# Turned spectra held in two Y tiles and one Z tile, moved within the next batch's first steps, with pd later and one x load behind a store

## The chip, the cores and the metric

The kernel runs on one core of one Trainium2 chip. The metric is the device time of one execution in microseconds (us). Before the change it is 518.89 us, the median of three runs (518.23 to 520.21).

## The reference

For each of B = 8 batches of 2496 tokens x 256 channels: a real FFT along the tokens, a complex linear layer on the spectrum, a soft threshold, and the inverse FFT. All 19,968 tokens then go through a soft mixture of experts with 32 slots.

```python
X = np.fft.rfft(x, axis=1)
Xr, Xi = (X.real.astype(np.float32), X.imag.astype(np.float32))
Yr = Xr @ w_r - Xi @ w_i + b_r
Yi = Xr @ w_i + Xi @ w_r + b_i
lam = 0.01
Yr = np.sign(Yr) * np.maximum(np.abs(Yr) - lam, 0.0)
Yi = np.sign(Yi) * np.maximum(np.abs(Yi) - lam, 0.0)
y = np.fft.irfft(Yr + 1j * Yi, n=2496, axis=1)          # becomes x below
logits = x @ phi                                        # 32 slots
slot_input = softmax(logits, axis=0).T @ x              # over all tokens
h = relu(slot_input[e] @ w1[e]); slot_out[e] = h @ w2[e]  # 8 experts, 4 slots each
out = softmax(logits, axis=1) @ slot_out
```

## The kernel before, in words

The FFT of length 2496 is split as 39 x 64. Each batch passes three stages, and the stages of neighbouring batches are interleaved on all engines.

- **a-units** (`a_unit`, 11 per batch). TensorE (PE) does the transform of length 39 on x. ScalarE (ACT) makes the high part `xh` of x, GpSimd (POOL) the low part `xl`, and three matmuls make `pa`. ACT copies it to `ast`, and four stores per batch bring it to DRAM (`adr`). The units of batch b run while batch b-1 is in its steps. Loads of x (`xr`, four columns each) go ahead of them.
- **steps** (`f2`, `lin_k`, `lin_y`, `tp_p`; five per batch, 40 in all). A step reads one fifth of `adr` back (`ap`), does the transform of length 64 (`px`), splits it (`xsm`, `xsh`, `xsl`, `xth`, `xtl`), does the linear layer (`pk`, `py`) and the threshold. The result `rt` (two per step, four buffers) goes to the logits (`pq`, `p_sb`).
- **chain of a batch** (`c_stages`, in the batch after). Logits back to tokens (`pg`, the round trip `gd`, `gp` through DRAM, `pL`), maxima, exponentials, then the slot weights back to the spectrum (`pe`, round trip `ed`, `eb`), and `pd`, whose halves need the split `chpd` (ACT) and `clpd` (POOL) of `eb`; `dd` is pd scaled. `slots_acc` then multiplies dd by the spectrum (`pr`).

For `pr` the spectrum is needed with frequency on the partitions. In the first three steps of a batch DVE transposes each `rt` in 32 x 32 blocks into `z` (tile Z, two buffers), and `z_move` sends 16 transfers of 96 KB from Z to `y` (tile Y, one buffer), which finish the turn. The two remaining steps are turned by PE (`pt`, `T`).

The order of the work is written by hand. Every piece is a generator that yields a planned time in units (four units are a step, 20 a batch), and a heap runs the pieces in the order of these times; each engine's instructions, and the transfers on SyncE's queue (SP), then stand in that order. The numbers come from the table `PLAN`: `zo` delays the transposes into z, `zd` and `z6` place the moves, `pd` places pd, `T_['wl']` the loads of the expert weights. All loads and stores in question go through the one queue of SP, in order.

After the 40 steps come the last batch's chain, the experts (`hps`, `po`) and the output (`pq` with `ost`, 41 stores).

Of the kernel before, what the change touches and what calls it, by code (L numbers as in the profile page):

```python
# [23 lines left out]
S = 32  # L24
# [40 lines left out]
def _constants():  # L65
# [87 lines left out]
    "pb": 9.8,  # L153
    "pe": [11.35, 12.35],
    "cm": 14.3,
    "pd": [17.12, 17.75],
    "pr": [20.48, 20.49, 24.48, 24.49, 28.49],
    "au": [1.4, 18.85, 19.7],
    "tho": 1.4,
# [72 lines left out]
def fourier_soft_moe_kernel(ctx: ExitStack, tc: tile.TileContext, t: dict, out: bass.AP):  # L232
# [159 lines left out]
    def a_unit(b, g, u):  # L392
# [170 lines left out]
    def lin_y(s, e):  # L563
        b, grp = steps[s]
        end = s == ns - 1
        t0 = 4 * s + 1 + (PLAN["T_"]["ye"] if end else 1.35) * e
        yield t0
        py = psum("pl", f"py{b}_{grp}_{e}")
        lin(py, e, 0, xts[(s, 0)], 4 * 64 if grp else WH)
        if e == 1 and not end:  # L570
            t0 = 4 * s + 3
            yield t0
        lin(py, e, 1, xts[(s, 1)], 4 * 64 if grp else WH)
        t0 += 0.55 if e == 0 else PLAN["T_"]["yt"] if end else 0.3
        yield t0
        ks = kss[s]
        ut = wtile([128, KG, 2, 64], F32, "ut", f"ut{b}_{grp}_{e}")
        for ri in range(2):
            V.scalar_tensor_tensor(
                out=ut[:, :, ri, :],  # L580
                in0=py[:, ri * 256 : ri * 256 + 256].rearrange("p (j q) -> p j q", q=64),
                scalar=bcol[:, ri, e : e + 1],
                in1=ks[:, e, :].rearrange("p (j q) -> p j q", q=64),
                op0=ALU.add, op1=ALU.add,
            )
        if s >= NZ + 2:
            rt = part("Z", 2, f"rt{b}_{grp}_{e}").rearrange("p (j c q) -> p j c q", c=2, q=64)
        else:
            rt = wtile([128, KG, 2, 64], F32, "rt", f"rt{b}_{grp}_{e}")
        yield t0 + (PLAN["T_"]["th"][e] if end else PLAN["tho"])  # L590
        relu = s < PLAN["hA"] or L_("th", s, e) is A
        if relu:
            A.activation(out=rt, in_=ut, func=AF.Relu, bias=nlam)
        else:
            P.tensor_scalar(out=rt, in0=ut, scalar1=LAM, scalar2=-LAM, op0=ALU.min, op1=ALU.max)
        yield t0 + (PLAN["T_"]["tl"][e] if end else PLAN["tlr" if relu else "tlo"])
        if relu:
            V.scalar_tensor_tensor(out=rt, in0=ut, scalar=LAM, in1=rt, op0=ALU.add, op1=ALU.min)
# [49 lines left out]
    def tp_t(s, h):  # L648
# [396 lines left out]
    def load_w(loc, layer):  # L1045
# [6 lines left out]
        if loc in "ZT":  # L1052
# [399 lines left out]
```

## Time and profile before

| | us |
|---|---|
| median of 3 runs | 518.89 (518.23 to 520.21) |
| profiled execution, its own time | 516.14 |
| its span, first to last instruction | 514.3 |
| PE busy | 489.8 (95%) |
| DVE busy | 358.0 (70%) |
| ACT busy | 328.8 (64%) |
| POOL busy | 311.7 (61%) |

Busy time is summed over one execution. A row of the timeline gives start and length of an instruction (or of several alike in a run), engine, line, operation, what it writes and reads, and in brackets the time its engine sat idle before it with what ended that. The line numbers are those of helpers that record most instructions, so the rows are told apart by the tiles' names, printed without batch numbers. A matmul's row is longer than the time to the next one's start, since matmuls are pipelined.

### The profile page before, as it was taken

The page shows a single profiled execution, that of the slowest core. Times are in us where ns is not written, and L with a number is a line of the kernel's source. Part 1 is how long each engine was busy: PE and PEld are TensorE (multiplying, and loading weights), DVE is VectorE, ACT ScalarE, POOL GpSimd, SP SyncE. Part 2 cuts the span into 40 slices and gives each one's busy share as a digit, 9 for nine tenths or more (in the row PEclk, how much of TensorE's full clock was granted, in tenths as well). Part 3 has the DMA queues.
Part 4 walks back from the last instruction along what each step waited for, and adds up shares of the span by engine and source line. Part 5 has one row for each costly group of instructions (what it writes and reads, how often), then busy time and mean ns, then how long its engine had stood idle before and what let it go on. Part 6 is the DMA issues. An engine that isn't in the chain of part 4 may idle for free. (4 is left out here: it accounts for less than half of the span.)

```text
span 514.3 us, 11973 instructions
## 1 busy us (share of the span) xinstructions
PE 489.8 (95%) x4348; PEld 418.7 (81%) x4348; DVE 358.0 (70%) x706; ACT 328.8 (64%) x718; POOL 311.7 (61%) x361
## 2 busy tenths in 40 slices
PE   8899999999999999999999999999999988999991
PEld 4487999999888978998898998989889866468881
DVE  3257876679667966887689868876896685437671
ACT  4357667768766876687668766775565456147771
POOL 0047587868985788689858985797367423313210
PEclk9899999999999999999999999999999999999997
DMA  8899656489857886888588867965889889939998
GB/s 291 281 322 352 215 185 205 125 260 244 282 127 249 237 273 151 259 237 291 146 258 244 264 169 210 259 233 162 243 203 337 219 244 385 349 121 397 403 406 346
DMA packets 90318, 130.98 MB, mean 255 GB/s; under 512 B 40188, under 2 KB 61692, under 8 KB 90260
## 3 DMA queue, kind: packets, MB, share of 16 engines
q1 hardware_dynamic: 89316, 128.10, 78.3%
q10 hardware_dynamic: 944, 2.13, 1.3%
q8 instruction: 34, 0.56, 0.4%
q14 instruction: 24, 0.20, 0.1%
HBM read 69.19 MB, written 50.00 MB: 232 GB/s over the span
## 5 line engine op out<-in xcount | busy, mean ns | idle before, releaser
L228 POOL TENSOR_TENSOR xl<-xr,xh 117x512 fp32r<-117x512 f32 x73 | 97.2, 1332 | 17.8 <-ACT xh L228 10.2
L304 PEld LDWEIGHTS px<-smov,ap 128*128 128x128 f32 x640 | 80.5, 192 | 6.3 <-issue 1.1
L304 PE MATMUL px<-smov,ap 128*128 128x128 f32 x640 | 84.2, 275 | 1.0 <-DMA ap<-adr 1.0
L228 DVE SCALAR_TENSOR_TENSOR ut<-py,pk,k 128x256 f32<-128x256 f32 x160 | 69.5, 475 | 19.6 <-PE py L304 17.4
L228 POOL TENSOR_TENSOR xsl<-xsm,xsh 128x256 fp32r<-128x256 f32 x77 | 72.1, 937 | 6.3
L228 POOL CAST xsh<-xsm 128x256 fp32r<-128x256 f32 x78 | 35.4, 453 | 66.5 <-DVE xsm L228 53.2
L228 ACT COPY ast<-pa 128x512 f32<-128x512 f32 x82 | 48.3, 591 | 35.4 <-PE pa L304 34.1
L228 DVE TENSOR_TENSOR xsm<-px,xsm 128x256 f32<-128x256 f32 x80 | 33.3, 417 | 40.0 <-ACT xth L228 35.4
L228 DVE TENSOR_TENSOR xtl<-px,xth 128x512 fp32r<-128x512 f32 x80 | 54.3, 679 | 0.1
L304 PE MATMUL py<-xth,nwsh 128*128 128x256 f32 (+1 forms) x160 | 52.9, 331 | 0.4 <-ACT k L228 0.4
L228 ACT CAST xth<-px 128x512 fp32r<-128x512 f32 x80 | 47.3, 592 | 5.4 <-PE py L304 5.3
L228 ACT CAST xh<-xr 117x512 fp32r<-117x512 f32 x72 | 45.3, 631 | 3.8 <-DMA xr<-in_x 3.8
L304 PE MATMUL pk<-xsh,w_rh 128*128 128x256 f32 (+1 forms) x160 | 47.6, 298 | 0.0
L228 POOL TENSOR_TENSOR rt<-ut,rt 128x512 f32<-128x512 f32 x36 | 46.3, 1285 | 0.1
L304 PE MATMUL pk<-xsl,w_rh 128*128 128x256 f32 (+1 forms) x160 | 45.0, 281 | 0.5 <-POOL xsl L228 0.3
L304 PE MATMUL py<-xth,wdh 128*128 128x256 f32 (+1 forms) x160 | 44.9, 281 | 0.0
L304 PE MATMUL py<-xtl,nwsh 128*128 128x256 f32 (+1 forms) x160 | 44.8, 280 | 0.0
L304 PE MATMUL py<-xtl,wdh 128*128 128x256 f32 (+1 forms) x160 | 44.7, 280 | 0.0
L304 PE MATMUL py<-xth,nwsl 128*128 128x256 f32 (+1 forms) x160 | 44.7, 279 | 0.0
L304 PE MATMUL pk<-xsh,w_rl 128*128 128x256 f32 (+1 forms) x160 | 44.7, 279 | 0.0
L304 PE MATMUL py<-xth,wdl 128*128 128x256 f32 (+1 forms) x160 | 44.6, 279 | 0.0
L228 ACT COPY xsm<-px 128x256 f32<-128x256 f32 x80 | 30.0, 375 | 22.6 <-PE px L304 15.2
(223 smaller groups left out, 1298.7 us busy)
## 6 DMA issues: line engine op xcount, KB each, us to landing
ap<-adr SPq DMA_DIRECT2D x76, 256.0 KB
out<-ost SPq DMA_DIRECT2D x37, 512.0 KB
xr<-in_x SPq DMA_DIRECT2D x35, 512.0 KB
adr<-ast SPq DMA_DIRECT2D x20, 768.0 KB
y<-z SPq DMA_DIRECT2D x112, 96.0 KB
w<-in_moe_w SPq DMA_DIRECT2D x21, 512.0 KB
adr<-ast SPq DMA_DIRECT2D x7, 512.0 KB
w<-in_moe_w SPq DMA_DIRECT2D x14, 256.0 KB
```

The source lines that it names most:

```text
L228: return lambda *a, **k: self.tc.keep_in_program_order(f(*a, **k))
L304: tc.keep_in_program_order(nc.tensor.matmul(**kw))
```

## The change

Z gets one buffer and Y two. The moves of a batch no longer wait for the next batch's middle: they stand at 14.9 to 26.6 units after the batch's start (before: 31 to 43.1; in batch 6 at 30.5 to 35). The first step's transposes into z come later (5.25 and 4.0 units instead of 2.2 and 0.7). `pd` moves from 17.12 and 17.75 to 18.9 and 19.2 in batches 0 to 4; batch 5 had these places already. The second load of x of a batch moves from 6 to 4.55 units ahead of its unit. Two weight loads go into Y (14.2 and 13.6 units before the end of the steps) instead of Z (6 and 5.9), the other loads of the table shift by up to 1.8 units, and small tiles at the end are taken from Y instead of Z or the other way round.

```diff
-    "pd": [17.12, 17.75],
+    "pd": [18.9, 19.2],
...
-    "zo": [2.2, 0.7, 1.0],
+    "zo": [5.25, 4.0, 0.7, 1.0],
...
-    "z6": [30.5, 0.3],
...
-    "zd": [31, 31.55, 32.1, 32.65, 33.2, 33.75, 34.3, 34.85, 35.4, 35.95, 36.5, 37.05, 41, 41.7, 42.4, 43.1],
+    "zd": [14.9, 15.4, 15.9, 21.2, 21.65, 22.1, 22.55, 23.0, 23.45, 23.9, 24.35, 24.8, 25.25, 25.7, 26.15, 26.6],
...
-    chain_bufs = {"ap": 3, "xth": 3, "xtl": 3, "xsh": 3, "xsl": 3, "Z": 2, "Y": 1, "T": 8, "p_sb": 2, "g_sb": 1,
+    chain_bufs = {"ap": 3, "xth": 3, "xtl": 3, "xsh": 3, "xsl": 3, "Z": 1, "Y": 2, "T": 8, "p_sb": 2, "g_sb": 1,
...
-            yield PLAN["x1"].get((b, g), tu - 6)
+            yield PLAN["x1"].get((b, g), tu - (4.55 if b > 1 and g == 4 else 6))
...
-            yield 20 * b + (PLAN["zd"][n] if b < B - 2 else PLAN["z6"][0] + PLAN["z6"][1] * n)
+            yield 20 * b + PLAN["zd"][n]
...
-            yield t0 + PLAN["tlo"] + PLAN["zo"][0 if grp == e == 0 else e + 1]
-            if grp == 0 and e == 0:
+            yield t0 + PLAN["tlo"] + PLAN["zo"][2 * (grp > 0) + e]
+            if b not in zts:
...
-            T = part("Z", 2, f"T{b}_{grp}_{h}")
+            T = part("Y", 2, f"T{b}_{grp}_{h}")
...
-            z = part("Z", 4, f"cin{b}")[:, : G * S].rearrange("p (g s) -> p g s", s=S)
+            z = part("Z" if b == 4 else "Y", 4, f"cin{b}")[:, : G * S].rearrange("p (g s) -> p g s", s=S)
```

What this does to the order shows at three places. In the rows below a name is the tile, its batch, and its column or step; the last number only tells buffers apart.

POOL, where pd of batch 4 meets the a-units of batch 7 (`xl7_14` is the low part for unit 14). Before:

```order
L228 TENSOR_TENSOR xl7_12_5074<-xr7_12_4913,xh7_12_5073 117x512
L228 TENSOR_TENSOR clpd4_0_5090<-eb4_4988,chpd4_0_5089 128x320
L228 TENSOR_TENSOR clpd4_1_5127<-eb4_4988,chpd4_1_5126 128x320
L228 TENSOR_SCALAR rt6_0_0_5080<-ut6_0_0_5077 128x512
L228 CAST xsh6_1_1_5119<-xsm6_1_1_5118 128x256
L228 TENSOR_TENSOR xsl6_1_1_5120<-xsm6_1_1_5118,xsh6_1_1_5119 128x256
L228 TENSOR_TENSOR rt6_0_0_5080<-ut6_0_0_5077,rt6_0_0_5080 128x512
L228 TENSOR_TENSOR dd4_4991<-dd4_4991,pk1_111 128x320
L228 TENSOR_TENSOR xl7_14_5164<-xr7_12_4913,xh7_14_5163 117x512
L228 TENSOR_TENSOR dd4_4991<-dd4_4991,pk1_111 128x320
```

Now:

```order
L227 TENSOR_TENSOR xl7_12_5082<-xr7_12_4921,xh7_12_5081 117x512
L227 TENSOR_SCALAR rt6_0_0_5088<-ut6_0_0_5085 128x512
L227 CAST xsh6_1_1_5124<-xsm6_1_1_5123 128x256
L227 TENSOR_TENSOR xsl6_1_1_5125<-xsm6_1_1_5123,xsh6_1_1_5124 128x256
L227 TENSOR_TENSOR rt6_0_0_5088<-ut6_0_0_5085,rt6_0_0_5088 128x512
L227 TENSOR_TENSOR xl7_14_5159<-xr7_12_4921,xh7_14_5158 117x512
L227 TENSOR_TENSOR clpd4_0_5178<-eb4_4996,chpd4_0_5177 128x320
L227 TENSOR_TENSOR clpd4_1_5197<-eb4_4996,chpd4_1_5196 128x320
L227 CAST xsh6_2_0_5207<-xsm6_2_0_5206 128x256
L227 TENSOR_TENSOR xsl6_2_0_5208<-xsm6_2_0_5206,xsh6_2_0_5207 128x256
L227 TENSOR_TENSOR dd4_4999<-dd4_4999,pk1_111 128x320
L227 TENSOR_TENSOR xl7_16_5252<-xr7_16_5075,xh7_16_5251 117x512
```

Both `clpd` and the first `dd` have gone from ahead of `xl7_14` to behind it. On PE the six matmuls of pd go the same way: the first three now stand between `pt` and `py` of the next step, the others behind that `py`, all ahead of the matmuls that read `xl7_14`.

SP, from the last store of batch 6's `adr` to the second fifth read back. Before:

```order
L298 DMA xr7_4_4590<-in_x 128x1024
L298 DMA adr6_3768<-ast6_18_4559 128x1024
L298 DMA y4_4645<-z4_3597 32x768 x4
L298 DMA ap6_0_4735<-adr6_3768 64x4x256 x2
L298 DMA y4_4645<-z4_3597 32x768
L298 DMA xr7_8_4748<-in_x 128x1024
L298 DMA y4_4645<-z4_3597 32x768 x2
L298 DMA ap6_1_4809<-adr6_3768 64x4x256 x2
```

Now:

```order
L297 DMA adr6_3783<-ast6_18_4575 128x1024
L297 DMA xr7_4_4659<-in_x 128x1024
L297 DMA ap6_0_4747<-adr6_3783 64x4x256 x2
L297 DMA xr7_8_4759<-in_x 128x1024
L297 DMA ap6_1_4818<-adr6_3783 64x4x256 x2
L297 DMA y5_4821<-z5_4537 32x768 x3
```

The store stands ahead of the load, and seven moves of batch 4 have left this place.

SP, in the last batch's steps, up to the round trip `gd6`, with loads of expert weights (`w`) between. Before:

```order
L298 DMA ap7_3_5909<-adr7_4592 64x4x256 x2
L298 DMA c_dr5_129<-cb5_5786 128x704
L298 DMA w5_5923<-in_moe_w2 128x1024
L298 DMA w6_5994<-in_moe_w2 128x1024
L298 DMA ap7_4_6034<-adr7_4592 64x4x256 x2
L298 DMA w7_6044<-in_moe_w2 128x1024
L298 DMA w8_6065<-in_moe_w2 128x1024
L298 DMA gd6_6072<-g_sb6_6001 64x20x32 x2
```

Now:

```order
L297 DMA ap7_3_5919<-adr7_4607 64x4x256 x2
L297 DMA y6_5619<-z6_5359 32x768
L297 DMA w5_5930<-in_moe_w2 128x1024
L297 DMA c_dr5_129<-cb5_5794 128x704
L297 DMA y6_5619<-z6_5359 32x768 x2
L297 DMA w6_5990<-in_moe_w2 128x1024
L297 DMA y6_5619<-z6_5359 32x768 x3
L297 DMA ap7_4_6050<-adr7_4607 64x4x256 x2
L297 DMA w7_6053<-in_moe_w2 128x1024
L297 DMA y6_5619<-z6_5359 32x768
L297 DMA w8_6074<-in_moe_w2 128x1024
L297 DMA gd6_6089<-g_sb6_6016 64x20x32 x2
```

Seven moves of batch 6 stand here that stood behind `gp6` before; six more stand between `eb5` and these rows, where four of batch 5 stood. Behind `gp6` all 16 moves are gone.

## Rows read from the trace of the kernel before

**Rows 1.** The page: busy time, share of the span, instructions.

```profile
PE 489.8 (95%) x4348; PEld 418.7 (81%) x4348; DVE 358.0 (70%) x706; ACT 328.8 (64%) x718; POOL 311.7 (61%) x361
```

**Rows 2.** Waits of PE: us in total, times, longest.

```profile
PE pa L304 <- POOL xl L228: 2.8, 4, 0.9
...
PE pr L304 <- DMA y<-z: 1.1, 1, 1.1
PE px L304 <- DMA ap<-adr: 1.0, 1, 1.0
```

**Rows 3.** Timeline of PE: start, length, engine, line, operation, [idle before it].

```profile
34.57 0.50 PE L304 MATMUL pa<-xl,f1h 117*128 117x512 f32 x1 [0.89 <-POOL xl L228]
...
341.24 0.40 PE L304 MATMUL pa<-xh,f1h 117*128 117x512 f32 x1
342.42 0.50 PE L304 MATMUL pa<-xl,f1h 117*128 117x512 f32 x1 [0.78 <-POOL xl L228]
```

**Rows 4.** Timelines of ACT and POOL ahead of that wait.

```profile
333.81 0.46 ACT L228 CAST chpd<-eb 128x320 fp32r<-128x320 f32 x1 [1.00 <-DMA eb<-ed]
...
334.34 0.87 POOL L228 TENSOR_TENSOR clpd<-eb,chpd 128x320 fp32r<-128x320 f32 x1 [1.33 <-ACT chpd L228]
...
340.64 1.73 POOL L228 TENSOR_TENSOR xl<-xr,xh 117x512 fp32r<-117x512 f32 x1
```

**Rows 5.** Timelines of PE and SP around the wait for ap.

```profile
317.37 1.13 PE L304 MATMUL px<-smov,ap 128*128 128x128 f32 x8 [0.98 <-DMA ap<-adr]
...
304.44 0.38 SPq L298 DMA_DIRECT2D adr<-ast  x1
304.91 3.58 SPq L298 DMA_DIRECT2D y<-z  x4
312.68 1.32 SPq L298 DMA_DIRECT2D ap<-adr  x2
```

**Rows 6.** Timelines of PE and DVE where pr of batch 6 begins.

```profile
425.49 1.50 PE L304 MATMUL pr<-y,dd 128*32 128x256 f32 x24 [1.13 <-DMA y<-z]
...
427.79 1.44 PE L304 MATMUL pL<-gp,pk 128*117 128x352 f32 x4
...
424.66 0.97 DVE L228 STREAM_TRANSPOSE gp<-gT 128x352 f32<-128x352 f32 x2
```

**Rows 7.** The chain of waits there: start, us, what.

```profile
420.69 4.57 DMA y<-z
```

**Rows 8.** Timelines of PE and POOL around pd of a batch without waits.

```profile
237.79 0.60 PE L646 MATMUL pt<-pk,rt 128*128 128x128 f32 x4
...
239.65 0.40 PE L304 MATMUL pa<-xh,f1h 117*128 117x512 f32 x1
239.88 0.39 PE L304 MATMUL pa<-xl,f1h 117*128 117x512 f32 x1
...
234.92 1.25 POOL L228 TENSOR_TENSOR xsl<-xsm,xsh 128x256 fp32r<-128x256 f32 x1
...
238.07 1.29 POOL L228 TENSOR_TENSOR xl<-xr,xh 117x512 fp32r<-117x512 f32 x1
```

**Rows 9.** Stretches: busy time of the engines, granted clock, DMA share, GB/s.

```profile
390.00:395.00 5.00, 5.00 (x67) 4.15 (x66) 2.11 (x5) 2.08 (x5) 4.31 (x7) 1.00 1.05 396
...
480.00:490.00 10.00, 10.00 (x55) 8.25 (x55) 7.34 (x12) 7.27 (x17) 2.32 (x3) 1.00 1.02 403
```

**Rows 10.** Timelines of SP and ACT around the round trip gd, gp of batch 6.

```profile
396.11 1.71 SPq L298 DMA_DIRECT2D gd<-g_sb  x2
...
405.43 0.24 ACT L228 COPY gp<-gp 40x64 f32<-40x64 f32 x1 [2.21 <-DMA gp<-gd]
```

**Rows 11.** Timelines of SP, DVE and POOL where z is next written.

```profile
239.39 0.33 SPq L298 DMA_DIRECT2D xr<-in_x  x1
...
248.12 0.71 DVE L228 STREAM_TRANSPOSE z<-rt 128x512 f32<-128x512 f32 x1 [1.94 <-POOL rt L228]
...
250.90 1.28 POOL L228 TENSOR_TENSOR xl<-xr,xh 117x512 fp32r<-117x512 f32 x1
```

More of the change, by code (lines that the diff above doesn't have):

```diff
@@ L168 @@
     "ws": [-29, -28.9, -28.8, 2],
-    "late": {'6': {'cms': [13.1, 13.2, 18, 22.65, 22.66, 22.67], 'pd': [16.681, 16.6], 'pdt': ('pl', 'pl'), 'pr': [17.15, 18.3, 20.179, 19.707, 19.902], 'pL': [6.6, 7.3], 'pm': 8.51, 'pmr': 9.35, 'pb': 10.36, 'pe': [11.747, 11.96, 12.419], 'pg': [0.875, 1.275], 'fr': {'sinv': 0, 'm2': 0, 'f1': 0, 'suni': 0}, 'pbx': 1.2, 'pet': ('pf', 'pf'), 'so': 0.2}, '5': {'pd': [18.9, 19.2], 'so': 1.5}, '4': {}},
-    "T_": {'wl': [[-31, 't', 1], [-29.5, 't', 1], [-27.7, 't', 1], [-25.5, 't', 1], [-23.7, 't', 1], [-21.7, 't', 2], [-20.2, 't', 2], [-19.2, 't', 2], [-18.7, 't', 2], [-18.2, 't', 2], [-15.2, 't', 2], [-14.3, 't', 2], [-13.4, 't', 2], [-12.5, 'c', 2], [-11.8, 's', 1], [-11.2, 'a', 1], [-10.6, 'a', 1], [-10, 'a', 1], [-9.5, 'Ww_r', 1], [-8.7, 'Wnws', 1], [-8.6, 'Wwd', 1], [-6, 'Z', 1], [-5.9, 'Z', 1], [0.01, 'k', 1], [0.01, 'u', 1], [0.02, 'x', 2], [0.02, 'x', 2], [0.02, 'x', 2], [1.4, 'R', 2], [1.4, 'R', 2], [1.73, 'Z', 2], [1.74, 'Z', 2]], 'cl': 2.0, 'cp': 46.5, 'ct': 46.6, 'du': [[2.55, 2]], 'd1': [], 'cm': [19.9, 19.91, 19.92, 25, 25.1, 25.2], 'cm7': [0.71, 1.7, 1.95, 2.7, 2.71, 2.8], 'ye': 0.2, 'te': [[5.6, 0.2], [5.5, 0.4]], 'pg': [-15.49, -11.49, -7.99, -3.934, -2.9], 'yt': 0.578, 'wr': -30.6, 'tp': [0, 0.6, 0.85, 0.5], 'tt': [0.4, 0.55, 0.821, 1.25, 0.994], 'z': 1.686, 'th': [0.1, 0.12], 'tl': [0.24, 0.25], 'pgt': ['ps', 'ps', 'ps', 'pf', 'pf'], 'ch': [0.263, 0.5, 0.7, 1.0, 1.514, 2.0], 'te7': 'AAAAAAAAAA', 'op': 2, 'ot': [3, 5, 7], 'gt': [-14.5, -10.5, -7.0, -3.93, -2.89]},
@@ new lines @@
+    "late": {'6': {'cms': [13.1, 13.2, 18, 22.65, 22.66, 22.67], 'pd': [16.681, 16.6], 'pdt': ('pl', 'pl'), 'pr': [17.15, 18.3, 20.179, 19.707, 19.902], 'pL': [6.6, 7.3], 'pm': 8.51, 'pmr': 9.35, 'pb': 10.36, 'pe': [11.747, 11.96, 12.419], 'pg': [0.875, 1.275], 'fr': {'sinv': 0, 'm2': 0, 'f1': 0, 'suni': 0}, 'pbx': 1.2, 'pet': ('pf', 'pf'), 'so': 0.2}, '5': {'so': 1.5}, '4': {}},
+    "T_": {'wl': [[-31, 't', 1], [-29.5, 't', 1], [-27.7, 't', 1], [-25.5, 't', 1], [-23.7, 't', 1], [-22, 't', 2], [-21, 't', 2], [-19.5, 't', 2], [-18.9, 't', 2], [-18.3, 't', 2], [-16.2, 't', 2], [-15.5, 't', 2], [-14.8, 't', 2], [-14.2, 'Y', 1], [-13.6, 'Y', 1], [-12.5, 'c', 2], [-11.8, 's', 1], [-11.2, 'a', 1], [-10.6, 'a', 1], [-10, 'a', 1], [-9.5, 'Ww_r', 1], [-8.7, 'Wnws', 1], [-8.6, 'Wwd', 1], [0.01, 'k', 1], [0.01, 'u', 1], [0.02, 'x', 2], [0.02, 'x', 2], [0.02, 'x', 2], [1.4, 'R', 2], [1.4, 'R', 2], [1.73, 'Z', 2], [1.74, 'Z', 2]], 'cl': 2.0, 'cp': 46.5, 'ct': 46.6, 'du': [[2.55, 2]], 'd1': [], 'cm': [19.9, 19.91, 19.92, 25, 25.1, 25.2], 'cm7': [0.71, 1.7, 1.95, 2.7, 2.71, 2.8], 'ye': 0.2, 'te': [[5.6, 0.2], [5.5, 0.4]], 'pg': [-15.49, -11.49, -7.99, -3.934, -2.9], 'yt': 0.578, 'wr': -30.6, 'tp': [0, 0.6, 0.85, 0.5], 'tt': [0.4, 0.55, 0.821, 1.25, 0.994], 'z': 1.686, 'th': [0.1, 0.12], 'tl': [0.24, 0.25], 'pgt': ['ps', 'ps', 'ps', 'pf', 'pf'], 'ch': [0.263, 0.5, 0.7, 1.0, 1.514, 2.0], 'te7': 'AAAAAAAAAA', 'op': 2, 'ot': [3, 5, 7], 'gt': [-14.5, -10.5, -7.0, -3.93, -2.89]},
@@ L1051, in load_w @@
             src = t["moe_w2"][e, h * 512 : h * 512 + 512, :].rearrange("(p f) d -> p (f d)", f=4)
-        if loc in "ZT":
+        if loc in "YZT":
             parts = [part(loc, 4, f"w{i}")]
```

## The prediction, on record before the changed kernel was timed

> **What bounds the kernel now.** I read the page's busy times first. PE works 489.8 us [rows 1] of a span of 514.3, so no change of order can be worth more than the 24.5 us in which it stands, and much of that lies in the start and behind the last matmul. None of PE's work changes: the two orders hold the same matmuls. So the question is which of PE's waits the change removes and which it makes. The second view is the table of PE's waits: three of its rows name something that the change touches, the low part `xl` from POOL (2.8 us in 4 waits), `y` from its moves (1.1), and `ap` read back from DRAM (1.0) [rows 2]. The timelines then give each wait its place and its cause. Of the four waits for `xl`, one of 0.89 us lies at 34.57, in the start, which the change doesn't touch [rows 3]; the other three, 1.9 us together, lie at one place of three batches, in unit 14, right behind `pd`.
>
> A row understates what such a wait costs. Where nothing is late the matmul on `xl` starts 0.23 us behind the one on `xh` (239.65, 239.88 [rows 8]); at 342.42 it starts 1.18 us behind (341.24, 342.42 [rows 3]). The loss is 0.95, the row says 0.78, because a matmul's row (0.40) is longer than its step. So I add 0.17 to each wait between pipelined matmuls.
>
> **The change, part by part.**
>
> *pd later.* The chain that makes `xl` late begins at a transfer. ACT waits 1.00 us for `eb` before it can cast `chpd`; POOL waits 1.33 us for that cast; its two `clpd`, three more instructions, a `dd` and then `xl` stand behind [rows 4], in the order that the rows of POOL show. `xl` is done at 342.37, and PE's matmul on it starts at 342.42. Now `eb` is asked for 1.8 units later, over 4 us (a unit is about 2.5 us: the `xh` matmul of unit 14 stands at 239.65 [rows 8] and two batches, 40 units, later at 341.24 [rows 3]), against a lateness of 1.0 to 1.3, and `xl` stands ahead of `clpd` and `dd` besides. I count all three waits as gone: 1.9 + 3 x 0.17 = **2.4 us**.
>
> It may put a new wait in their place, since PE now needs `clpd` soon behind `xl`. I walk through a batch without waits [rows 8]. POOL finished `xl` at 239.36. Two `clpd` (0.87 each [rows 4]), about 0.2 between them and one `dd` (0.7) leave its front, so it would be done near 236.7, and the first `clpd` at 237.6. POOL can't use all of that time, as its `xsh` also waits for DVE; the gap that opens I put at up to 0.6, which moves `clpd` to 238.1. PE ended the four `pt` at about 238.15 (237.79 and four steps); pd's six matmuls, about 1.0 us, leave its front, so it comes to pd's first matmuls at 237.15 and to the third, which reads `clpd`, near 237.5. The miss is between 0.1 and 0.6; with a short `xsl` (some 0.5 less than the row's 1.25) it is nothing. It would come in five batches. Batch 5 has this order already and its pd is in no row of the waits, but no a-unit runs there to load POOL. I take 0.15 a batch, 0.75 in all, and keep 0 and 3.0 as bounds.
>
> The length of POOL's instructions there decides that. The Trainium skill (SBUF — State Buffer, "Who interferes with whom") says that a DVE instruction with two SBUF inputs and a GpSimd instruction that reads SBUF share a port pair which one of them holds while the other blocks. The row of 1.25 us for an `xsl` agrees with such a block; by that rule every late `clpd` would cost its upper bound, 0.6 in five batches, 3.0 us.
>
> *x behind adr's last store, and seven moves gone there.* The first fifth `ap` of a batch can be read only when the last store of `adr` has landed. At 304.44 that store was issued, behind a load of x; four moves followed it until 308.49; then SP stood until it could issue `ap` at 312.68, and PE waited 0.98 us for it [rows 5]. Now 512 KB of x no longer stand ahead of the store. At 396 GB/s, the rate of a full queue [rows 9], that is 1.3 us, and the store is issued about 0.4 earlier. 1.7 us is more than the wait of 0.98 + 0.17, so I count **1.15 us**. The load of x itself moves one place back; its reader, `xh`, runs some 6 us later, and the seven moves that shared the queue with it (0.7 MB) are gone. I cost it at nothing; without that cover it would be the same 1.3 us once.
>
> *Moves at once, in the last batch.* Before `pr` of batch 6 PE waits 1.13 us [rows 6] for a move that was issued at 420.69 and took 4.57 us [rows 7]. The moves now stand some 25 us earlier, so this goes. What is late next: `dd` is there, since the `pz` that reads it ran ahead of `pr`. Behind `pr` stands `pL`, at 427.79, and its input is complete at 425.63 (424.66 + 0.97), so it can start 1.13 us earlier too [rows 6]. **1.13 us**, without the 0.17, as nothing was in the pipeline.
>
> *The price in the last batch.* Between `eb5` and `gd6` SP now issues 13 moves instead of 4. The queue is full there (share 1.05 at 396 GB/s [rows 9]), and `gd6`, `gp6` stand behind: ACT already waits 2.21 us for `gp` [rows 10], and `pL` of batch 6 on PE follows at once. Nine moves of 96 KB are 0.88 MB, 2.2 us at that rate. Lower bound nothing: 16 moves of batch 5 have left the 45 us before, and SP spreads the new ones over 10 us. I take 0.5, nearer to the lower end, as the queue enters this stretch with less behind it.
>
> *At nothing:* the weight loads, whose reader is the expert stage (two come some 20 us earlier, the rest shift by under 5 us; no wait of PE names them); the transposes of step 0, which keep their length and DVE is busy 358 us of 514 [rows 1]; the small tiles at the end.
>
> **The sum.** 2.4 + 1.15 + 1.13 - 0.75 - 0.5 = 3.4 us. The profiled execution took 516.14, of which 1.84 lie outside its span; it becomes 512.7 (span 510.9). The median of the runs is 2.75 above that execution, and I carry the difference over: 518.89 - 3.4 = **515.5 us**.
>
> **The rivals.**
>
> *The waits move (same).* `clpd` is late in five batches (3.0), `gd6` by the full 2.2: 4.7 - 5.2 = -0.5, so 519.4; half of both gives 516.8. For it: the miss at `clpd` is worked out so close to zero, and ACT's 2.21 us. Against it: batch 5's clean pd. The Trainium skill (DMA: Bandwidth & Descriptors, "Queues, rings and completion order") says that each engine takes the descriptors of a queue in ring order; by that rule `gd6` pays for all nine moves, and the full 2.2 us stand. No run here has yet shown it.
>
> *One Z tile is too few (slower).* Batch 4's first transpose into z at 248.12 now writes the tile from which batch 3's moves read. The last three of these are issued behind the load of x that stood at 239.39 [rows 11]; with ten moves instead of four ahead I put the last at about 242. At 4.57 us each [rows 7] it lands at 246.6, 1.5 us early. If it lands later, DVE stands with everything behind it, and the two transposes of step 0 (0.71 each) now stand there too. `xsm`, POOL's `xsl` and then `xl` (250.90 to 252.18) follow; I put the slack of that `xl` at some 3 us, 1.8 with the two transposes. So it decides from a landing about 8 us after issue; each further us costs PE one in each of six batches. At 9 us: +6 - 3.4 = +2.6, so 521.5. Against it: transfers of 96 KB have taken under 5 us in a full queue.
>
> *The end is set by the stores (same).* From 470 on the DMA engines are at share 1.02 and PE at 100% together [rows 9]. If the output's stores were the bound from their beginning, an earlier PE would only fill the queue sooner. But they can't begin before the experts are done, and DMA is far from full in the 10 us ahead, so this holds only if weights are late: 518.5.
>
> **How the numbers follow.** Forecast (2.6 us or more gained) 0.53; waits move 0.26; stores 0.08; Z too few 0.13. A measurement can tell about 0.5%, 2.6 us: faster is below 516.3, slower above 521.5. So faster 0.53, same 0.34 (the two middle cases), slower 0.13. The range: at the low end all 4.7 us and, since the timed runs were 2.75 longer than the profiled one and may hold more waits for transfers of the same kind, that too: 511.5. At the high end the first rival's 519.4 and a little of the third case: 520.0. The forecast's own range is 511.5 to 516.3.
>
> **What would show it.** Right: no wait for `xl` behind pd in the batches, no wait for `y` ahead of pr, none for `ap` at a batch's first `px`; a span near 511. The first rival shows as waits of PE at `pd` for POOL `clpd` and at `pL` for `gp`. One Z tile too few shows as DVE's transposes waiting for a DMA `y<-z`, and late `xsm` behind them. The forecast is wrong if the three waits go and others of the same length stand in the steps, where a batch without waits already has POOL only half a us ahead of PE (239.36 against 239.88).

## The result: slower by 0.8%

| | before | changed |
|---|---|---|
| median (22 executions each) | 519.12 us | 522.33 us |
| ratio, 95% interval | | 1.0082 [1.0057, 1.0106] |
| profiled execution, its own time | 516.14 us | 522.65 us |
| its span | 514.3 us | 520.9 us |

The forecast was 515.5 us with a range to 520.0. The time lies above the range, on the other side of no change.

PE's work is what it was. The page of the changed kernel (busy time, share, instructions) answers [rows 1]:

```profile
PE 489.7 (94%) x4348; PEld 419.4 (81%) x4348; DVE 362.6 (70%) x706; ACT 330.4 (63%) x718; POOL 312.6 (60%) x361
```

So the 6.6 us of longer span are not added work. The table of PE's waits (us in total, times, longest) in the changed kernel:

```profile
PE pL L303 <- DMA gp<-gd: 3.8, 1, 3.8
PE pd L303 <- POOL clpd L227: 3.2, 5, 0.6
...
PE pL L303 <- DVE clpL L227: 1.6, 2, 1.1
...
PE pa L303 <- POOL xl L227: 0.9, 1, 0.9
```

The waits of [rows 2] that the change was to remove are gone: `y` ahead of `pr`, `ap` at a batch's first `px`, and all waits for `xl` but the one in the start. Two others stand in their place: `gp`, once, and `clpd`, five times.

Where each costs time shows when the execution is cut at the matmul `pm`, which stands once in each batch. First the timeline of PE before, `pm` of batches 0, 5 and 6, and then the same for the changed kernel with the two kinds of new wait.

```profile
110.22 0.32 PE L768 MATMUL pm<-pk,mx 117*128 117x117 f32 x1
...
365.59 0.32 PE L768 MATMUL pm<-pk,mx 117*128 117x117 f32 x1
...
412.03 0.32 PE L768 MATMUL pm<-pk,mx 117*128 117x117 f32 x1 [0.51 <-ACT gT L228]
```

```profile
109.98 0.32 PE L767 MATMUL pm<-pk,mx 117*128 117x117 f32 x1
...
237.94 0.42 PE L303 MATMUL pd<-clpd,sunih 128*128 128x320 f32 x1 [0.65 <-POOL clpd L227]
...
366.19 0.32 PE L767 MATMUL pm<-pk,mx 117*128 117x117 f32 x1
...
411.16 1.51 PE L303 MATMUL pL<-gp,pk 120*128 120x352 f32 x2 [3.80 <-DMA gp<-gd]
415.03 0.95 PE L303 MATMUL pL<-gp,pk 120*128 120x352 f32 x2
...
419.33 0.32 PE L767 MATMUL pm<-pk,mx 117*128 117x117 f32 x1 [0.51 <-ACT gT L227]
```

| start of pm to start of pm, us | before | changed | difference |
|---|---|---|---|
| batch 0 to 5 | 255.37 | 256.21 | +0.84 |
| batch 5 to 6 | 46.44 | 53.14 | +6.70 |
| batch 6 to the end of the span | 102.27 | 101.57 | -0.70 |

In the five batches the waits removed (1.91 for `xl`, 0.98 for `ap`) and the waits made (3.25 at `pd`) nearly cancel; small waits at `pL` (0.42 before, 0.64 and 0.49 now) make up most of the rest. The loss of the profiled execution lies in the last batch, at one wait.

The medians differ by 3.2 us and not by 6.5. The first trace of before is a short one in this place, which may explain that. It has no wait for `gp` in batch 6; three other traces with the moves late, from the experiments below, have one of 0.77, 1.26 and 1.64 us. From `pm` of batch 5 to the end of the span the first trace takes 148.71 us and those three 152.65, 152.52 and 150.34; the changed kernel takes 154.71, and its variants that keep the last batch 153.32 to 155.45.

**The wait at pd.** Timelines of DVE and POOL in the changed kernel around the `pd` at 237.94:

```profile
234.27 1.63 DVE L227 TENSOR_TENSOR cb<-cb,cs 128x704 f32<-128x704 f32 x1
...
233.89 1.27 POOL L227 TENSOR_TENSOR rt<-ut,rt 128x512 f32<-128x512 f32 x1
235.12 1.95 POOL L227 TENSOR_TENSOR xl<-xr,xh 117x512 fp32r<-117x512 f32 x1
237.02 2.16 POOL L227 TENSOR_TENSOR clpd<-eb,chpd 128x320 fp32r<-128x320 f32 x2
```

`xl`, now ahead of `clpd`, takes 1.95 us; in [rows 8] it took 1.29. The difference, 0.66, is PE's wait of 0.65. It is 1.94 or 1.95 in all five batches. DVE's product `cb<-cb,cs` takes 1.63 to 1.66 in all six batches; in the trace before it took 0.88 to 1.06 in batches 0 to 4, where other work of POOL stood beside it:

```profile
234.69 0.89 DVE L228 TENSOR_TENSOR cb<-cb,cs 128x704 f32<-128x704 f32 x1
```

The rows also tell who holds whom. `cb` starts at 234.27, while POOL's `rt` runs (233.89 to 235.16), and ends 0.74 us behind the end of `rt`. `xl` starts at 235.12, while `cb` runs, and ends 1.17 us behind the end of `cb` (235.90). Over the five batches these distances are 0.74 to 0.76 and 1.15 to 1.17. So the one that starts later gets almost nowhere until the earlier has ended: `cb` loses its time to `rt`, and `xl` loses its own to `cb`. With its 0.88 us `cb` would have ended at 235.15, just as `xl` starts.

**The wait for gp.** SP's queue in the changed kernel from the loads behind `eb5` to `gp6` (answers [rows 10]):

```profile
382.21 1.82 SPq L297 DMA_DIRECT2D y<-z  x3
...
384.70 2.56 SPq L297 DMA_DIRECT2D y<-z  x3
...
389.13 0.61 SPq L297 DMA_DIRECT2D y<-z  x1
...
392.05 1.20 SPq L297 DMA_DIRECT2D y<-z  x2
...
393.93 2.17 SPq L297 DMA_DIRECT2D y<-z  x3
...
398.86 0.57 SPq L297 DMA_DIRECT2D y<-z  x1
...
400.51 2.35 SPq L297 DMA_DIRECT2D gd<-g_sb  x2
...
407.52 1.06 SPq L297 DMA_DIRECT2D gp<-gd  x3
```

SP's own waits between 380 and 401, before:

```profile
SPq L298 <- ACT g_sb L228: 4.4, 1, 4.4
```

In the changed kernel the same view has no wait for `g_sb`; its first row is

```profile
SPq L297 <- DMA w<-in_moe_w: 2.5, 3, 1.2
```

There a load of weights that was issued earlier has to land first. What one move holds SP for is in the view of the tile `y`, before (min, median and max in ns, first and last start):

```profile
L298 SPq DMA_DIRECT2D y<-z x112: 507/590/1678, 100.8 to 420.7; - x112
```

Before, SP stood 4.4 us with nothing to issue until `g_sb` was ready, and `gd6` went out at 396.11 [rows 10]. Now SP is late: `gd6` goes out at 400.51, and SP issues `gp`, which needs gd landed, 7.01 us behind it (before 401.47 - 396.11 = 5.36). Counted from `pm` of batch 5, `gd6` is 3.80 us later (34.32 against 30.52). Between `eb5` and `gd6` the 13 moves hold SP for 8.6 us in sum where the four of before held it for 2.2; the 4.4 us in which it stood are used up, and it stands some 2 us more for earlier transfers to land. The longer landing is not shown to come from the change: in the three other traces with the moves late it takes 6.66 to 7.18 us.

The price goes beyond the wait. Windows of the changed kernel (busy time by engine, then granted clock, DMA share, GB/s):

```profile
401.00:406.00 5.00, 5.00 (x68) 4.18 (x67) 2.11 (x6) 1.57 (x5) 1.12 (x3) 1.00 1.03 265
406.00:411.00 5.00, 1.05 (x6) 0.64 (x5) 0.00 (x0) 0.00 (x0) 1.80 (x2) 0.76 0.69 203
411.00:416.00 5.00, 4.84 (x18) 4.10 (x19) 2.25 (x5) 2.56 (x6) 1.64 (x2) 0.56 0.92 330
416.00:421.00 5.00, 4.49 (x60) 3.91 (x60) 4.23 (x8) 2.03 (x6) 2.25 (x3) 1.00 1.04 381
```

While PE stands, the granted clock falls (0.5 is the level of 1.2 GHz, 1.00 that of 2.4), and it stays low for most of the 5 us behind the stall. The `pL` pair takes 1.51 us (0.76 in kernels without the stall), and from `pL` to `pm` it is 8.17 us; before it was 412.03 - 405.91 = 6.12. So 6.70 is 3.80 of wait, 2.05 of slow clock, and 0.85 in smaller pieces.

### The profile page after: what moved, and what is told of

It reads as the page before. It is cut to its first block, busy times and chain, and to the rows that moved or that the text cites. A ratio compares the mean times of both kernels' runs of the same rounds, so it can differ in the third digit from the quotient of the medians.

```text
span 520.9 us, 11962 instructions
## 1 busy us (share of the span) xinstructions
PE 489.7 (94%) x4348; PEld 419.4 (81%) x4348; DVE 362.6 (70%) x706; ACT 330.4 (63%) x718; POOL 312.6 (60%) x361
## 4 chain that ended last, share of the span: by engine, by line
PE 71%; DMA 10%; DVE 6%; POOL 5%; ACT 3%; SPq 2%; issue 1%; ACTq 0%; DVEq 0%; POOLq 0%
PE py L303 17%; PE px L303 10%; PE pq L303 10%; PE pa L303 9%; PE pk L303 6%; PE pr L303 3%; DMA y<-z 3%; PE pt L645 3%; POOL xl L227 3%; DMA gd<-g_sb 2%; SPq L297 2%; PE pL L303 2%; PE pc L645 2%; DMA gp<-gd 2%; DMA xr<-in_x 2%; PE pe L303 1%
## 5 line engine op out<-in xcount | busy, mean ns | idle before, releaser
L227 POOL TENSOR_TENSOR xl<-xr,xh 117x512 fp32r<-117x512 f32 x73 | 98.9, 1355 | 17.8 <-ACT xh L227 9.2
L227 POOL CAST xsh<-xsm 128x256 fp32r<-128x256 f32 x78 | 32.9, 422 | 72.6 <-DVE xsm L227 59.4
```

Source lines behind the costliest of these rows:

```text
L227: return lambda *a, **k: self.tc.keep_in_program_order(f(*a, **k))
```

## The experiments

Theory: two separate losses, (1) `xl` and DVE's `cb` in each other's way, which makes `clpd` late in five batches, and (2) SP too far behind for `gd6` because of the moves of batch 6. Rivals: for (1) that the order on POOL alone makes `clpd` late; for (2) that the bytes of the moves and not their issues delay the round trip. The ratios are to the kernel before, measured on the same chip.

| kernel | median us | ratio [95%] | pm 0 to 5 | pm 5 to 6 | pm 6 to end |
|---|---|---|---|---|---|
| changed | 522.33 | 1.0082 [1.0057, 1.0106] | 256.21 | 53.14 | 101.57 |
| cb behind rt | 520.62 | 0.9995 [0.9962, 1.0029] | 251.79 | 52.41 | 101.35 |
| cb as a reduction | 519.33 | 1.0012 [0.9976, 1.0048] | 251.83 | 51.86 | 101.46 |
| pd back | 523.45 | 1.0082 [1.0049, 1.0114] | 255.61 | 53.68 | 101.77 |
| ten moves behind gp6 | 534.68 | 1.0296 [1.0261, 1.0330] | 255.24 | 63.24 | 101.59 |
| moves of batch 6 by ACT | 521.27 | 1.0038 [1.0013, 1.0063] | 255.60 | 51.14 | 101.92 |
| moves of batch 6 halved, twice as many | 528.76 | 1.0172 [1.0121, 1.0222] | 255.00 | 58.72 | 101.39 |
| weights behind gp6 | 515.93 | 0.9922 [0.9891, 0.9953] | 255.42 | 46.37 | 101.51 |
| weights behind gp6, cb behind rt | 514.06 | 0.9891 [0.9847, 0.9936] | 253.18 | 46.36 | 101.62 |
| before, pd alone | 519.74 | 0.9997 [0.9961, 1.0034] | 256.36 | 47.38 | 105.27 |
| before, x load alone | 517.48 | 0.9969 [0.9928, 1.0010] | | | |
| before, pd, x load, cb behind rt | 514.81 | 0.9920 [0.9890, 0.9951] | 252.32 | 47.87 | 104.65 |

### cb behind rt

```diff
-        s_ = steps or [PLAN["cm"] + d for d in (0, 0.5, 1.3, 2.3, 3.1, 3.8)]
+        s_ = steps or [PLAN["cm"] + d for d in (0, 0.5, 1.3, 2.3, 5.0, 5.5)]
```

> The changed kernel with one edit: DVE's product cb<-cb,cs of batches 0 to 5 stands behind the rt of the step instead of ahead of xsm. Theory 'two instructions in each other's way': in the changed kernel cb takes 1.64 us instead of 0.88, and the xl that follows on POOL 1.95 instead of 1.28; the second stretch of 0.67 is the wait of 0.65 at pd. So cb moved: xl ahead of clpd takes 1.28 to 1.30, the five waits of PE at pd for clpd fall from 0.65 to under 0.1 each, and the time falls by about 5 x 0.8 = 4 us. Rival 'only the order on POOL': clpd is late because it stands behind xl at all; cb's place does nothing, five waits of about 0.65 stay, and the time is that of the changed kernel.

No wait for `clpd` is left. POOL's timeline in this kernel, the `xl` ahead of `clpd`:

```profile
232.23 1.29 POOL L227 TENSOR_TENSOR xl<-xr,xh 117x512 fp32r<-117x512 f32 x1
233.48 1.70 POOL L227 TENSOR_TENSOR clpd<-eb,chpd 128x320 fp32r<-128x320 f32 x2
```

The five batches are 256.21 - 251.79 = 4.42 us shorter, 0.88 for each `pd`, and the ratio falls from 1.0082 to 0.9995. The order on POOL is the same, so that rival falls. The wait for `gp` stays (4.17).

### cb as a reduction

```diff
-        (P if b >= B - 2 else V).tensor_tensor(out=cb, in0=cb, in1=cs.broadcast_to([n, G, S]), op=ALU.mult)
+        if b >= B - 2:
+            P.tensor_tensor(out=cb, in0=cb, in1=cs.broadcast_to([n, G, S]), op=ALU.mult)
+        else:
+            V.tensor_reduce(out=cm, in_=cb, axis=AX.X, op=ALU.max)
```

> The changed kernel with DVE's product cb<-cb,cs of batches 0 to 5 replaced, at the same place, by a reduction of the same tile (cm<-cb, 0.88 us as the one that makes cs): one large input in SBUF in place of two. The weights that combine the slots are left unscaled. Theory 'port pair', after the Trainium skill (SBUF, Who interferes with whom: two SBUF inputs on DVE contend with GpSimd, a tensor_reduce never does): the reduction takes 0.88, xl takes 1.28 to 1.30 instead of 1.95, and the five waits of 0.65 at pd fall under 0.1; time about 4 us less than the changed kernel. Rival 'any work of DVE beside it' or 'the order on POOL alone': xl stays at 1.9 or the waits stay at 0.6.

Timelines of DVE and POOL, the same place:

```profile
233.63 0.88 DVE L227 TENSOR_REDUCE cm<-cb 128x22 f32<-128x704 f32 x1
...
234.48 1.30 POOL L227 TENSOR_TENSOR xl<-xr,xh 117x512 fp32r<-117x512 f32 x1
```

An instruction of DVE as long as an undisturbed `cb`, at the same place, leaves `xl` at 1.28 to 1.31, and no wait stands at `pd`. The reduction runs beside `rt` (233.25 to 234.52) and is not held by it; it has ended (234.51) as `xl` starts. So it is not DVE's being busy that costs, but what `cb` reads or writes: the reduction has one large input in place of two and writes 22 columns in place of 704, which this run does not separate. What a reduction does beside `xl` itself is not tested. The Trainium skill (SBUF — State Buffer, "Who interferes with whom") says that a DVE instruction with two inputs in SBUF contends with a GpSimd instruction that reads SBUF, and that a reduction never does on trn2; `cb` and the reduction beside `rt` both agree.

### pd back

```diff
-    "pd": [18.9, 19.2],
+    "pd": [17.12, 17.75],
```

(and batch 5 keeps 18.9 and 19.2).

> The changed kernel with pd of batches 0 to 4 back at its old place. Theory: the five waits for clpd (0.65 each, with the restart about 0.8) go, and the waits for xl behind pd in three batches (1.9 us, with the restart 2.4) come back: time 1.5 to 2 us less than the changed kernel. Rival: without the old moves in SP's queue eb comes earlier, so that the waits for xl stay away too: 4 us less.

The waits for `clpd` go and three for `xl` behind `pd` come back (0.46, 0.73 and 0.34), as PE's waits show (four, one of them that of the start):

```profile
PE pa L303 <- POOL xl L227: 2.4, 4, 0.9
```

The time is that of the changed kernel, 1.0082: the first expectation's gain of 1.5 to 2 us is not seen (the five batches are 0.6 us shorter), and the second's 4 us still less. Alone, in these tiles, moving `pd` was worth nothing that the interval (about 1.7 us) can show.

### Before, with pd moved alone

```diff
-    "pd": [17.12, 17.75],
+    "pd": [18.9, 19.2],
```

> The kernel before with pd of batches 0 to 4 at its new place, nothing else. The three waits for xl behind pd (1.9 us) go. Theory: cb and POOL's xl meet here as in the changed kernel, cb takes about 1.64, xl 1.95, and five waits of 0.65 stand at pd: in sum 1 to 1.5 us slower than the kernel before. Rival: the meeting comes from the new places of the transposes into z; then no wait stands at pd and the time is 2 us less.

Timelines of PE and DVE in that kernel:

```profile
237.78 0.42 PE L304 MATMUL pd<-clpd,sunih 128*128 128x320 f32 x1 [0.64 <-POOL clpd L228]
...
234.12 1.64 DVE L228 TENSOR_TENSOR cb<-cb,cs 128x704 f32<-128x704 f32 x1
```

`cb` and `xl` meet here too (1.64 and 1.95), with five waits of 0.64 to 0.65, so it is `pd`'s place and not the new tiles. The three waits for `xl` are gone, and the ratio is 0.9997: no gain of this part is seen. The expected loss of 1 us cannot be told from that.

### Before, with the x load alone

```diff
-            yield PLAN["x1"].get((b, g), tu - 6)
+            yield PLAN["x1"].get((b, g), tu - (4.55 if b > 1 and g == 4 else 6))
```

> The kernel before with the second load of x of a batch behind adr's last store, nothing else. Theory: no wait for ap at the first px of a batch (1.0 us in the kernel before), the other waits as before: 1 us less, 0.2%. Rival: seven moves of y stay in that queue, so ap still comes late and nothing changes.

Its trace, used for this one wait alone, shows none for `ap`. The ratio of 0.9969 holds the expected 0.998 and 1.0 both; this part is too small to be told by its time.

### Ten moves of batch 6 behind gp6

```diff
-            yield 20 * b + PLAN["zd"][n]
+            yield 20 * b + (PLAN["zd"][n] if b < B - 2 or n < 6 else 30.5 + 0.3 * (n - 6))
```

> The changed kernel with ten of the 16 moves of batch 6 behind gp6 (only six stand early, three of them between eb5 and gd6). Theory 'SP and its queue are behind': in the changed kernel gd6 is issued 4.4 us later than before and lands 1 us slower; with the moves gone gd6 is issued where g_sb is ready (near 396.5), PE's wait of 3.8 us for gp and the low granted clock behind it (0.76, 0.56) are gone, and the time falls by about 6 us. The wait for y ahead of pr of batch 6 stays away, as ten moves are fewer than the 16 of before. Rival 'weights and ap fill that queue anyway': gd6 stays 3 us or more late and the time falls by under 2 us.

The issue is on time, as the theory has it: SP issues `gd6` at 400.03, where it stood for `g_sb` (30.46 us behind `pm` of batch 5, as before), and `gp` 4.64 us behind. But the time rises by 2% over the changed kernel. Timelines of PE and POOL, then the windows:

```profile
422.83 0.58 PE L303 MATMUL pk<-xsh,w_rh 128*128 128x256 f32 x1 [13.55 <-POOL xsh L227]
...
421.81 0.61 POOL L227 TENSOR_SCALAR rt<-ut 128x512 f32<-128x512 f32 x1 [17.95 <-DMA w_cl<-in_moe_w]
```

```profile
411.00:416.00 5.00, 0.00 (x0) 0.00 (x0) 0.02 (x1) 0.00 (x0) 0.00 (x0) 0.56 1.04 320
416.00:421.00 5.00, 0.00 (x0) 0.00 (x0) 0.00 (x0) 0.00 (x0) 0.00 (x0) 0.50 1.05 290
```

`xsh` stands behind POOL's `rt` of step 2 of batch 7. From there on the code puts `rt` into tile Z (`rt = part("Z", 2, ...)` for the last steps), and with one Z that is the tile from which batch 6 is moved, so `rt` has to wait for the last move, issued at 414.73 to 416.78. The row names `w_cl`, a load that is issued behind those moves; by the trace's semaphores POOL had stood until then for landings of `y<-z`, at 416.33 and 421.50, and `w_cl` came 0.24 us later. That the moves hold Z fits the code. Early moves in batch 6 are therefore a need of one Z tile, which neither the forecast nor this expectation saw.

### Moves of batch 6 halved, twice as many

```diff
+            for h in range(2 if b == B - 2 else 0):
+                sp(
+                    out=yts[b][32 * j : 32 * j + 32, i, h].rearrange("p k x -> p (k x)"),
+                    in_=zts[b][32 * i : 32 * i + 32, j, h].rearrange("p k x -> p (k x)"),
+                )
+            if b == B - 2:
+                continue
```

> The changed kernel with each of the 16 moves of batch 6 sent as two of 48 KB: the same bytes at the same places, twice the issues. Theory S, SP's time for the issues: the 13 moves between eb5 and gd6 become 26, 13 more at 0.5 to 0.6 us, so gd6 is issued 6 to 8 us later still and PE's wait for gp grows from 3.8 us to about 10. Theory B, the bytes in the queue: gd6 stands where it stands in the changed kernel, the wait for gp stays near 4 us.

The same bytes cost 58.72 - 53.14 = 5.6 us more from `pm` to `pm`. SP issues `gd6` at 404.59; counted from `pm` of batch 5 that is 40.0 us, and 34.3 in the changed kernel, 5.7 later for 13 more issues. The wait for `gp` does not grow to 10, though, since PE is held up ahead of it:

```profile
404.62 1.13 PE L303 MATMUL px<-smov,ap 128*128 128x128 f32 x8 [1.94 <-DMA ap<-adr]
409.20 0.58 PE L303 MATMUL pk<-xsh,w_rh 128*128 128x256 f32 x1 [2.26 <-POOL xsh L227]
415.16 1.51 PE L303 MATMUL pL<-gp,pk 120*128 120x352 f32 x2 [3.92 <-DMA gp<-gd]
```

What a move of 48 KB holds SP for is in the view of `y` from 360 to 405 us:

```profile
L297 SPq DMA_DIRECT2D y<-z x32: 507/589/1518, 361.0 to 403.3; - x32
```

Half the bytes hold SP as long (0.59 in the median, as for 96 KB). So theory S holds (issues cost SP time) and theory B's "nothing changes" falls.

### Moves of batch 6 issued by ACT

```diff
-            sp(
+            (sp if b < B - 2 else aq)(
```

> The changed kernel with the 16 moves of batch 6 issued by ACT at the same places, the same transfers in another queue. Theory S, the time that SP takes to issue them (nine more at 0.6 us are 5.4 us): gd6 is issued near 396.5 again, PE's wait for gp falls from 3.8 us to under 1, time about 5 us less, minus what 0.6 us for each issue costs ACT and those who wait for it. Theory B, the traffic: gd6 is issued on time but gd and gp still land late by the time of the extra 0.88 MB (2.2 us), so about 2 us of wait for gp stay.

No wait for `gp` is left, and the 2 us that theory B kept do not stand. `gd6` is not issued near 396.5, though, but at 401.16: SP stands 2.9 us for `g_sb`, which is late because PE is, at `pd`. It goes out as soon as `g_sb` is ready (in the changed kernel 3.9 us behind that), and `gp` follows after 4.65 us. ACT pays instead. The view of `y`, a piece of the chain of waits, and the timelines of ACT and PE:

```profile
L300 ACTq DMA_DIRECT2D y<-z x16: 514/558/674, 366.3 to 397.3; - x16
...
381.18 8.45 DMA w<-in_moe_w
...
390.87 0.46 ACT L227 CAST chpd<-eb 128x320 fp32r<-128x320 f32 x1 [5.56 <-DMA y<-z]
...
391.38 0.41 PE L303 MATMUL pd<-chpd,sunih 128*128 128x320 f32 x1 [2.93 <-ACT chpd L227]
```

ACT issues three moves from 386.07 to 390.83, and `chpd` stands behind them. The issues take 1.66 us of these 4.76; for 3.05 us ACT stands ahead of the second, by the chain for a load of weights that SP issued at 381.18 and that landed 8.45 us later. So part of the gain moves to `pd`. As PE is late there, the round trip has more time beside it, and this run alone would not separate S from B; the one before it does.

### Weights behind gp6

```diff
-[-22, 't', 2], [-21, 't', 2], [-19.5, 't', 2], [-18.9, 't', 2], [-18.3, 't', 2],
+[-17.2, 't', 2], [-17.1, 't', 2], [-17, 't', 2], [-16.9, 't', 2], [-16.8, 't', 2],
```

> The changed kernel with five loads of expert weights (512 KB each) put behind gp6; four of them stood between eb5 and gd6, one between gd6 and gp6. The moves of batch 6 stay early. If gd6 is late because SP's queue holds too much ahead of it, four issues fewer (2.4 us) and 2 MB less bring gd6 forward by 2 to 4 us and its landing from 7.0 to about 5 us: the wait of 3.8 us for gp falls under 1 and the low clock behind it goes, 5 us or more off the time. Rival: the weights are then late where the experts begin, and the time comes back there as PE's waits for w.

SP's and PE's timelines at the round trip:

```profile
399.08 1.92 SPq L297 DMA_DIRECT2D gd<-g_sb  x2
...
403.54 1.06 SPq L297 DMA_DIRECT2D gp<-gd  x3
...
408.67 0.76 PE L303 MATMUL pL<-gp,pk 120*128 120x352 f32 x2
```

`gp` follows 4.46 us behind `gd6`, `pL` has no wait, its pair takes 0.76 again, and the stretch is 46.37, as in the first trace of before. PE's stretch behind `pm` of batch 6 is no longer than in the changed kernel (101.51), so the rival (weights late) falls. 1.0082 becomes 0.9922: 1.6% or 8.3 us, more than the 6.77 of the stretch, but within the two intervals. It takes the loads as well as the moves to make SP late: with four loads fewer ahead, `gd6` goes out 30.66 us behind `pm` of batch 5, as before, and the moves stay.

### Weights behind gp6 and cb behind rt

```diff
-[-22, 't', 2], [-21, 't', 2], [-19.5, 't', 2], [-18.9, 't', 2], [-18.3, 't', 2],
+[-17.2, 't', 2], [-17.1, 't', 2], [-17, 't', 2], [-16.9, 't', 2], [-16.8, 't', 2],
...
-        s_ = steps or [PLAN["cm"] + d for d in (0, 0.5, 1.3, 2.3, 3.1, 3.8)]
+        s_ = steps or [PLAN["cm"] + d for d in (0, 0.5, 1.3, 2.3, 5.0, 5.5)]
```

> Both mends in the changed kernel, the five loads behind gp6 and cb behind rt: if the two losses are separate, their gains add, about 4 us for pd and 5 us for gp: 9 us less than the changed kernel, so about 1% less than the kernel before. Rival: with PE 4 us earlier at batch 6, gd6 is as late as ever beside it and less than half of the second gain is seen.

The two gains stand together in the trace: no wait for `clpd`, none for `gp`. 514.06 us, 0.9891 of the kernel before, is the fastest of these kernels, and 1.9% (9.9 us) below the changed kernel, as expected. But the interval does not separate it from 0.9922, and the five batches are 2.24 us shorter than with the loads alone, where `cb` alone gave 4.42: that the gains add in full is not shown.

### Before, with pd, the x load and cb

```diff
-    "pd": [17.12, 17.75],
+    "pd": [18.9, 19.2],
...
-            yield PLAN["x1"].get((b, g), tu - 6)
+            yield PLAN["x1"].get((b, g), tu - (4.55 if b > 1 and g == 4 else 6))
...
-        s_ = steps or [PLAN["cm"] + d for d in (0, 0.5, 1.3, 2.3, 3.1, 3.8)]
+        s_ = steps or [PLAN["cm"] + d for d in (0, 0.5, 1.3, 2.3, 5.0, 5.5)]
```

> The kernel before (two Z, one Y, the moves late) with three edits alone: pd at its new place, the load of x behind adr's last store, and cb behind rt. If the gains forecast for these two parts of the change are real without the new tiles, the waits for xl behind pd (1.9 us) and the wait for ap (1.0 us) go, nothing stands at pd, and the time is 3 to 3.5 us (0.6%) less than the kernel before. Rival: the waits removed come back elsewhere in the steps and the time is that of the kernel before.

No wait for `xl` behind `pd`, for `clpd` or for `ap` is left, and the ratio is 0.9920, a little more than forecast. What stands are two waits of the last batch:

```profile
403.46 0.83 PE L304 MATMUL pL<-gp,pk 120*128 120x352 f32 x2 [1.26 <-DMA gp<-gd]
...
423.30 2.76 PE L304 MATMUL pr<-y,dd 128*32 128x256 f32 x24 [1.31 <-DMA y<-z]
```

Behind the second wait `pr` takes 2.76 us (1.50 in [rows 6]), and the stretch behind `pm` of batch 6 is 104.65. The granted clock is 0.84 and 0.82 in the two windows of 5 us from 420 on; in the first trace of before it is 1.00 in both. In this execution the late `y`, which the changed kernel no longer has, costs more than the 1.13 us that the forecast counted.

### The kernel before once more

> The kernel before once more, unchanged, for a second trace of it. Its profiled execution took 516.14 us, its median is near 519. Theory: the last batch's round trip and y run close to late in it already, as gp is waited for 0.8 to 1.3 us and y 1.3 to 1.6 in kernels that share that part with it; so another execution shows such waits in batch 6, 1 to 3 us from pm of batch 5 to pm of batch 6 above the 46.4 of the first trace. Rival: the difference lies in the start, which differs by some us between executions of all kernels, and batch 6 shows 46.4 again.

PE's timeline at `gp` of batch 6:

```profile
406.48 0.83 PE L304 MATMUL pL<-gp,pk 120*128 120x352 f32 x2 [1.64 <-DMA gp<-gd]
```

From `pm` 5 to 6 it is 48.31 us, 1.87 more than in the first trace: the round trip was already at its limit before the change. `y` is not waited for in this trace, so the expected wait for it is not seen. Its time, 516.53, is nearly as low as that of the first trace all the same, as the start (by 0.71), the five batches (by 0.52) and the end (by 0.24) were shorter; so where the 2.75 us between the profiled execution and the median lie is only partly shown.

## Why the prediction failed, step by step

- **The waits for xl (2.4 us forecast).** Right: 1.91 us in three batches are gone.
- **ap (1.15).** Right in the trace: 0.98 us is gone, in the changed kernel and with the load alone.
- **y ahead of pr in batch 6 (1.13).** Right: gone, and the stretch behind `pm` of batch 6 is 0.70 shorter. In two other traces with the moves late that stretch is 104.65 and 105.27, so the usual gain may be larger.
- **clpd late at pd (0.15 a batch, 0.75 in all; bounds 0 and 3.0).** The mechanism was named, the size was off: 0.65 a batch, 3.25 in all, and 4.4 by the experiment that removes it. The walk let POOL run `xl` in the 1.29 us of [rows 8]. At its new place it starts while DVE's `cb` runs, which `rt` has held up, and takes 1.95. The text looked for a block at `xsl`, not at the instruction whose place the change itself had put beside `cb`; what stands on DVE at that time was not looked up. In the trace this part gave back more than the first gained, and before with `pd` alone no gain is seen (0.9997).
- **The price in the last batch (0.5; bounds 0 and 2.2).** This step failed. It priced nine moves by their 0.88 MB alone. SP needs about 0.59 us to issue one (median of 112), so nine are 5.3 us, against the 4.4 us in which SP had stood; both numbers were in the trace of before. In the run the nine took 6.4 us more, SP stood some 2 us for earlier transfers to land, and `gd6` went out 3.80 us later. PE's wait of 3.80 us for `gp` and 2.05 us of low clock behind it, for which the text had no term, make most of the 6.70 us. The doubled moves show that the number of issues costs; how much of SP's standing the bytes cause is open. Against the three other traces with the moves late (47.38 to 48.31 from `pm` to `pm`) the price is 4.8 to 5.8 us.
- **The rivals.** "The waits move" was the right one in kind, at both of its places, and too small: 3.25 for 3.0 and 6.7 for 2.2. "One Z tile is too few" fell as it was put: DVE's transposes into z wait for POOL's `rt` alone (14.2 us in 8 waits, none for a transfer). The need of early moves in batch 6 is where one Z tile does bind. "The end is set by the stores" fell: behind `pm` of batch 6 all kernels with the new tiles take 101.3 to 101.9 us, however early PE comes there. The rule on ring order was given 2.2 us for `gd6`. No run shows it as a cost of the nine moves: the landing takes 7.01 us now and 5.36 in the first trace, but 6.66 to 7.18 in three others with the moves late; what is later is the issue.

## What to carry to other kernels

A transfer put ahead of a round trip costs the queue's issue time as well as its bytes: add up the issues and hold the sum against the time that the issuing engine stands before that round trip. When an instruction moves on GpSimd, look up what VectorE runs as it starts, and the other way round: here the one that started later stood until the earlier had ended, and the delay passed from `rt` to `cb` to `xl`. Add a term for the granted clock to a forecast stall of TensorE: 3.80 us of wait cost 6.70 here. And take more than one trace of the kernel before, as a wait that one execution misses by little is there in others.

## What the runs showed of the hardware

- DVE's `cb` (0.88 us at best) takes 1.64 when it starts 0.38 us into POOL's `rt` (1.27), and the `xl` that then starts beside `cb` takes 1.95 (1.28 at best): the later one ends 0.74 to 0.76 (`cb`) or 1.15 to 1.17 us (`xl`) behind the end of the earlier. A reduction of the same tile as `cb` takes 0.88 beside the same `rt`.
- After the stall of 3.80 us the clock was at 0.76 and 0.56 in two windows of 5 us, after 13.55 us at 0.50. With the stalls of 2.93 and 0.39 of the moves by ACT the windows stayed at 1.00; with the wait of 1.31 us for `y` (before with three edits) they fell to 0.84 and 0.82. So the length of a stall alone does not tell its price.
- One move of 96 KB holds SP for at least 0.51 us, 0.59 in the median, and one of 48 KB as long; on ACT one of 96 KB takes 0.56 in the median.
- `pm` of batch 0 stands between 109.5 and 114.3 us in fourteen traces of these kernels, so a single span says little to under 1%.
